# Moving a PSUM copy, one set of loads and the last stores in a Fourier-and-feed-forward kernel

## The chip, the cores and the metric

The kernel runs on one core of a Trainium2 chip. The metric is the device time of one execution in microseconds; several executions are taken and their median is compared. The profile is of one further execution.

## The reference

The input x has 8 batches of 3008 rows and 256 columns, in float32. Each batch gets a two-dimensional discrete Fourier transform, of which the real part is kept, and the result goes through a feed-forward layer with a hidden width of 2048 and the activation h cos(h):

```python
X = np.fft.fft(np.fft.fft(x, axis=1), axis=2).real
h = X.reshape(24064, 256) @ w_in        # 256 -> 2048
out = (h * np.cos(h)) @ w_out           # 2048 -> 256
```

## The kernel before, in words

The length 3008 is split into 47 x 64. For each batch a *transform* runs in two halves. The first half folds the rows of x (pairs of rows and pairs of columns are added and subtracted, so that cosines and sines need half the products), multiplies by a 47-point matrix (`first_half`, eight chunks c = 0 to 7 of the 64 residues) and writes the result to a buffer in DRAM (`store_z`). `load_z` reads it back in another order, and the second half (`second_half`, six groups g) multiplies by the 64-point matrix and gives a tile pq per group. The column transform is merged into the feed-forward weights (WC, WS), so pq goes straight into the feed-forward part.

The feed-forward part is a software pipeline of 384 steps t (8 batches, 6 groups, 8 slices fp of the hidden width, two blocks of 128 each). A step has seven matmuls of the second product into four PSUM accumulators M (`mm2`, L730), four of the first product into H (`mm1`, L640), and on the other engines: a seed of H from the norm row nb on ACT (`seed`, L610), a difference on DVE (`dve_h`, L656), rounding on ACT (`act_round`, L671), the fraction on DVE (`dve_frac`, L675), the sine on ACT (`act_sin`, L681), products on DVE (`dve_g`, L685) and three sums on DVE (`dve_s` with k = 0, 1, 2; L696 and L706). Each engine runs its instructions in the written order of the loop `for t in range(n + LAG + 1)` at the end of the kernel. Where a step is the last slice of its group, ACT copies the accumulators out (`take_m`), GpSimd adds them over the next four steps (`combine_m`, `add`), and seven and eight steps after that slice the two halves of the output tile are transposed on DVE and stored (`store_out`, L826 and L836).

The next batch's transform is laid between these steps. `transform(b)` enters its calls under the number of the step at whose end they run (`todo`), before whose sums they run (`between`), or beside which sum GpSimd starts (`aside`). For the second batch (b = 1) the loads of x (`load_later_x`, L178) stand at steps 2 to 5 for the first half of the columns p = 0 (tile xp0) and at 13 to 16 for p = 1. A call issues seven DMAs of up to seven rows; a fourth of a half has 28. Half of the calls read rows in ascending order, 8 KB at a stretch; the other half reads them in reversed order, 1 KB at a stretch. SP issues them, as it issues the edge rows xz (`load_ends`, L183), the norm row's way through DRAM (`second_half`, pq to nd, nd to nb, L495 and L496) and nearly all stores.

The first half for batches after the first is `first_half_later`. Chunks c = 0 and c = 4 begin with `middle_later`: eight or nine small matmuls (L341, L349) for column 128, the middle one, into columns 256 to 272 of the PSUM tile pz, and a copy of them on ACT into the tile mid (L352). Then come the wide products (L373 for c = 0, L385 for all) into columns 0 to 256 of pz and into a spare half of an accumulator, and ACT copies both and a few columns of mid into zs (L394 to L396). There are 7 such batches, so L352 runs 14 times.

The last step has its own ending. `combine_last` forms the last group's sums on DVE (L794 to L801), and `store_last` transposes them on PE (L811), copies them to ob (two buffers, in turn with those of `store_out`) and stores each half with four DMAs of 64 KB: six of the eight on SP, two on ACT (L818).

Of the kernel before, what the change touches and what calls it, by code (L numbers as in the profile page):

```python
# [30 lines left out]
LAG = 3  # L31
# [102 lines left out]
def kernel(  # L134
# [7 lines left out]
    nc = tc.nc  # L142
# [9 lines left out]
    x_r = x.rearrange("b (s2 s1) d -> b s2 s1 d", s1=64)  # L152
# [11 lines left out]
    def load_later_x(b, p, s, set_):  # L164
        i0 = 16 * set_ + 8 * p
        skip = 1 if s and i0 == 0 else 0
        cols = slice(64 - i0 - skip, 56 - i0, -1) if s else slice(i0, i0 + 8)
        to = xs[p].rearrange("r (s i d) -> r s i d", s=2, d=ND)[:, s, skip:8]
        for k in range(7):
            if s:  # L170
                r0, n = max(0, 40 - 7 * k), 5 if k == 6 else 7
                rows, p0 = slice(r0, r0 + n), 64 * set_ + _turned(46 - r0)
                part = slice(p0, p0 + n)
            else:
                n = 7 if k < 5 else 6
                rows, p0 = slice(k, N2, 7), 64 * set_ + 6 - k
                part = slice(p0, p0 + 7 * n - 6, 7)
            nc.sync.dma_start(out=to[part], in_=x_r[b, rows, cols])  # L178

    def load_ends(b):  # L180
        for set_ in range(2):
# [60 lines left out]
    mid = cpool.tile([128, NI], FP, tag="mid", name="mid")  # L242
# [92 lines left out]
    def middle_later(pz, p):  # L335
        pm = pz[64:128, 256:272]
        for set_ in range(2):
            i0 = 1 if set_ == p == 0 else 0
            for s in range(2):
                xm = xs[p].rearrange("r (s i d) -> r s i d", s=2, d=ND)[0:XL, s, i0:8, 128]  # L340
                nc.tensor.matmul(  # L341
                    pm[:, 8 * set_ + i0 : 8 * set_ + 8],
                    lhsT=weights(2 + set_, 0, XL),
                    rhs=xm,
                    start=s == 0,
                    stop=s == 1,
                )
        if p == 0:
            nc.tensor.matmul(  # L349
                pm[:, 0:1], lhsT=weights(4, 0, XL), rhs=xz[0:XL, 128:129], start=True, stop=True  # L350
            )
        nc.scalar.copy(  # L352
            out=mid[64:128].rearrange("y (h p i) -> y h p i", h=2, p=2)[:, :, p],
            in_=pm.rearrange("y (h i) -> y h i", h=2),
        )

    def clear_spare():
        nc.scalar.activation(
# [7 lines left out]
    def first_half_later(b, c):  # L366
        pz = psum("pz")
        spare = acc[live[0]][3][:, 256:512]
        if c % 4 == 0:
            middle_later(pz, c // 4)  # L370
        if c == 0:
            for e in range(2):
                nc.tensor.matmul(  # L373
                    pz[64 * e : 64 * e + 64, 0:128],
                    lhsT=weights(4 + e, 0, XL),
                    rhs=xfz[0:XL, 128 * e : 128 * e + 128],
                    start=True,
                    stop=True,
                )
        xf = xf1[c % 2]  # L380
        for e in range(2):
            for set_ in range(2):
                r0, r1 = 64 * set_, 64 * set_ + XT
                c0 = 128 if set_ == c == 0 else 0
                nc.tensor.matmul(  # L385
                    (spare if set_ else pz)[64 * e : 64 * e + 64, c0:256],
                    lhsT=weights(e, r0, r1),
                    rhs=xf[r0:r1, 256 * e + c0 : 256 * e + 256],
                    start=set_ == 0,
                    stop=True,  # L390
                    skip_group_check=set_ == 1,
                )
        zs = spool.tile([128, 512], FP, tag="zs", bufs=4, name="zs")
        nc.scalar.copy(out=zs[:, 256:512], in_=spare)  # L394
        nc.scalar.copy(out=zs[:, 0:256], in_=pz[:, 0:256])
        nc.scalar.copy(  # L396
            out=zs[64:128, 0:512:128].rearrange("y (h i) -> y h i", h=2),
            in_=mid[64:128].rearrange("y (h i) -> y h i", h=2)[:, :, 2 * c : 2 * c + 2],
        )
        zss[b, c] = zs  # L400
# [105 lines left out]
    todo = {}  # L506
# [3 lines left out]
    def transform(b):  # L510
        t0 = (b - 1) * NG * 8

        def at(o, *call):
            todo.setdefault(t0 + o, []).append(call)

        for p, o in enumerate((2, 13) if b == 1 else (-20, -9)):
            for k in range(4):
                at(o + k, load_later_x, b, p, k % 2, k // 2)
        at(4 if b == 1 else -16, load_ends, b)
        for c in range(NCH):  # L520
            o = 7 + 8 * (c // 2) + 2 * (c % 2)
            f = o + 2 + c % 2
            for e in range(2):
                aside.setdefault(t0 + o + e, []).append((fold_rows, b, c, e))
                between.setdefault(t0 + o + e + 1, []).append(
                    (fold_cols, xf1[c % 2], xs2[e], e)
                )
            at(f - 1, clear_spare)
            at(f, first_half, b, c)
            at(f + 1, store_z, b, c, 0)  # L530
            at(f + 1, store_z, b, c, 1)
        for e in range(2):
            between.setdefault(t0 + 7 + e, []).append((fold_cols, xfz, xz, e))
        at(38, load_z, b, 0)
        at(38, load_z, b, 1)
        for g, o in enumerate((42, 44, 46, 49, 52, 55)):
            at(o, second_half, b, g)
# [266 lines left out]
    def store_last(s, sg):  # L804
        cv = outs[s.b, s.grp].rearrange("p (m t) -> p m t", m=7)
        ob = spool.tile([128, 512], FP, tag="ob", bufs=2, name="ob")
        ov = ob.rearrange("t (h c j) -> t h j c", h=2, j=2)
        pos = [psum("po", "H").rearrange("t (z j c) -> t z j c", z=2, j=2)[:, 0] for _ in "ab"]
        for j in range(2):
            for h in range(2):  # L810
                nc.tensor.transpose(  # L811
                    pos[h][:, j], cv[:, 2 * sg + j, 128 * h : 128 * h + 128], ident
                )
        nc.scalar.copy(out=ov[:, 0], in_=pos[0])
        (nc.vector.tensor_copy if sg else nc.scalar.copy)(out=ov[:, 1], in_=pos[1])
        for t0, j, k, m in sorted(_runs(s.grp, sg)):
            h, r0 = divmod(32 * t0, 128)
            (nc.scalar if sg and h else nc.sync).dma_start(  # L818
                out=out_r[s.b, j, k : k + m, :],
                in_=ob[r0 : r0 + m, 256 * h : 256 * h + 256],  # L820
            )
# [78 lines left out]
    def step(t, last=None):  # L900
        s = steps[t] if 0 <= t < n else None
        return s if s is not None and (last is None or s.fp == 7) else None
# [10 lines left out]
    for t in range(n + LAG + 1):  # L913
        cur, prev, old, done = step(t), step(t - 1), step(t - 2), step(t - LAG)
        if cur:
            mm1(cur, 0)
            act_e(cur)
            if t == 0:
                spread_norm()
            if t in early:  # L920
                fold_weights(*early[t])
        if t - LAG - 1 == n - 1:
            combine_last(steps[n - 1])
            break
        if step(t - LAG - 1, True):
            take_m(step(t - LAG - 1), 1)
            combine_m(step(t - LAG - 1))
        if done:
            live[0] = (done.b, done.grp)
            mm2(done, 0)  # L930
        if old:
            dve_g(old, 0)
        if step(t + 1):
            seed(step(t + 1))
        if prev:
            dve_frac(prev, 0)
        if old:
            dve_g(old, 1)
        if prev:
            dve_frac(prev, 1)  # L940
            act_sin(prev)
        if old:
            dve_s(old, 0)
        for call in between.pop(t, ()):
            call[0](*call[1:])
        if done:
            dve_s(done, 2)
        ahead = dve_s(old, 1) if old else None
        if step(t - LAG, True):
            take_m(done, 0)  # L950
        if cur:
            mm1(cur, 1)
        if done:
            mm2(done, 1)
        if cur:
            dve_h(cur)
            act_round(cur, 0)
            act_round(cur, 1)
        for call in aside.pop(t, ()):
            beside(call[0](*call[1:]), ahead)  # L960
        if step(t - LAG - 4, True):
            store_out(step(t - LAG - 4), 0)
        if step(t - LAG - 5, True):
            store_out(step(t - LAG - 5), 1)
        for call in opening.pop(t, ()):
            call[0](*call[1:])
        for call in todo.pop(t, ()):
            call[0](*call[1:])
# [30 lines left out]
```

## Time and profile before

| what | value |
|---|---|
| median of 3 runs | 1966.43 us (1965.71 to 1967.67) |
| profiled execution | 1966.13 us, span 1964.4 us |
| granted TensorE clock, mean | 0.997 |
| PE, DVE, ACT, POOL busy | 1926.7, 1782.5, 1531.3, 379.6 us |
| matmuls of the second product, M (L730) | 7 per step, 384 steps |
| copies of the middle column (L352) | 14 x 0.17 us |
| loads of x by `load_later_x` (L178) | 392, on SP |

Times in the profile count from the start of the span. PE is the matmul unit, PEld its weight loads, DVE, ACT and POOL the vector, scalar and GpSimd engines; a q behind a name is the engine's queue, where DMAs are issued. A line of the timeline gives start, duration, engine, line of the kernel, operation and tiles; brackets hold the idle time just before and what ended it.

### The profile page before, as it was taken

How to read it: one execution, taken by the hardware profiler on the slowest of the kernel's cores; microseconds unless marked ns; L12 is line 12 of the kernel's file. 1: busy time of each engine (PE TensorE's matmuls, PEld its weight loads, DVE VectorE, ACT ScalarE, POOL GpSimd, SP SyncE). 2: the span in 40 equal slices, each digit the busy share in tenths (PEclk: the TensorE clock that was granted, in tenths of full speed). 3: DMA queues.
4: the chain of work that ended last, by engine and by line, in shares of the span. 5: the costliest groups of instructions: out<-in, count | busy, mean ns of one | idle time of the engine just before them, and what ended most of it. 6: DMA issues, size and time to landing. Idle time of an engine off the chain costs nothing.

```text
span 1964.4 us, 30495 instructions
## 1 busy us (share of the span) xinstructions
PE 1926.7 (98%) x9524; PEld 1690.4 (86%) x9524; DVE 1782.5 (91%) x3343; ACT 1531.3 (78%) x2881; POOL 379.6 (19%) x434
## 2 busy tenths in 40 slices
PE   7899999999999999999999999999999999999998
PEld 3788889888998889988898888988889888898887
DVE  4899998999899998999989999899999999999997
ACT  3687878877788788787877888778877888788775
POOL 2122202222022211222112221122211222111100
PEclk8999999999999999999999999999999999999999
DMA  6221130012200121101211122110231000110000
GB/s 198 95 57 37 49 91 25 19 38 68 64 23 22 41 75 52 25 24 46 80 39 26 26 52 76 33 31 22 54 84 29 24 23 24 53 29 10 12 22 22
DMA packets 159931, 89.31 MB, mean 45 GB/s; under 512 B 108298, under 2 KB 154114, under 8 KB 157302
## 3 DMA queue, kind: packets, MB, share of 16 engines
q1 hardware_dynamic: 158282, 86.27, 16.6%
q8 instruction: 76, 1.25, 0.3%
q10 hardware_dynamic: 1392, 1.05, 0.2%
q14 instruction: 85, 0.70, 0.1%
q0 software_dynamic: 96, 0.05, 0.0%
HBM read 50.04 MB, written 37.28 MB: 44 GB/s over the span
## 4 chain that ended last, share of the span: by engine, by line
PE 84%; DVE 7%; issue 3%; DMA 2%; ACT 2%; SPq 1%; DVEq 0%; ACTq 0%; POOL 0%; POOLq 0%
PE M L730 50%; PE H L640 30%; PE pb L473 2%; PE pz L385 2%; DVE r L685 1%; ACT r L671 1%; DVE S L696 1%; DVE h L656 1%; DMA xp<-in_x_dram 1%; DVE r L675 1%; DVE S L706 1%; DVE ob L826 1%; DMA zd<-zs 1%; DMA out_dram<-ob 1%; SPq L836 1%
## 5 line engine op out<-in xcount | busy, mean ns | idle before, releaser
L730 PE MATMUL M<-S,VX 128*128 128x256 f32 (+1 forms) x2304 | 612.3, 375 | 0.0
L730 PEld LDWEIGHTS M<-S,VX 128*128 128x128 f32 x2304 | 437.8, 190 | 49.9
L671 ACT ACTIVATE r<-H 128x512 f32<-128x512 f32 (+1 forms) x384 | 226.2, 589 | 264.8 <-DVE h L656 264.8
L681 ACT ACTIVATE r<-r 128x1024 f32<-128x1024 f32 (+1 forms) x384 | 394.8, 1028 | 21.6 <-DVE r L675 16.7
L640 PE MATMUL H<-pq,WC 128*128 128x256 f32 (+1 forms) x1536 | 394.6, 379 | 4.2 <-ACT H L610 4.2
L640 PE MATMUL H<-pq,WS 128*128 128x256 f32 (+1 forms) x1536 | 388.2, 375 | 0.6 <-ACT ew L651 0.5
L730 PE MATMUL M<-r,w 128*128 128x256 f32 (+1 forms) x1536 | 387.7, 375 | 0.0
L610 ACT ACTIVATE H<-nb,wn 128x256 f32<-128x256 f32 (+1 forms) x766 | 362.9, 474 | 18.4 <-DMA nb<-nd 4.5
L656 DVE TENSOR_TENSOR h<-ew,H 128x512 f32<-128x512 f32 (+1 forms) x384 | 258.7, 674 | 119.0 <-PE H L640 75.6
L640 PEld LDWEIGHTS H<-pq,WC 128*128 128x128 f32 x1536 | 283.3, 190 | 54.9 <-issue 11.1
L730 PEld LDWEIGHTS M<-r,w 128*128 128x128 f32 x1536 | 300.2, 196 | 27.4
L640 PEld LDWEIGHTS H<-pq,WS 128*128 128x128 f32 x1536 | 291.9, 190 | 36.6 <-ACT ew L651 1.8
L675 DVE SCALAR_TENSOR_TENSOR r<-r,H 128x512 f32<-128x512 f32 (+1 forms) x384 | 258.6, 673 | 28.0 <-ACT r L671 11.4
L651 ACT ACTIVATE ew<-H 128x512 f32<-128x512 f32 (+1 forms) x384 | 225.7, 588 | 56.4 <-PE H L640 47.3
L696 DVE TENSOR_TENSOR S<-r 128x512 f32<-128x512 f32 (+1 forms) x384 | 259.7, 676 | 0.1
L685 DVE SCALAR_TENSOR_TENSOR r<-H,r 128x512 f32<-128x512 f32 (+1 forms) x384 | 255.7, 666 | 4.4 <-ACT r L681 4.0
L782 POOL TENSOR_TENSOR cb<-cb,mr 128x256 f32<-128x256 f32 (+3 forms) x188 | 158.3, 852 | 519.5 <-DVE S L706 484.8
L675 DVE SCALAR_TENSOR_TENSOR r<-r,h 128x512 f32<-128x512 f32 (+1 forms) x384 | 258.3, 673 | 0.0
L685 DVE SCALAR_TENSOR_TENSOR r<-h,r 128x512 f32<-128x512 f32 (+1 forms) x384 | 258.0, 672 | 0.0
L671 ACT ACTIVATE r<-h 128x512 f32<-128x512 f32 (+1 forms) x384 | 236.0, 615 | 0.0
L300 POOL TENSOR_TENSOR xs<-xp 113x512 f32<-113x512 f32 x112 | 143.0, 1277 | 460.5 <-DVE S L706 403.7
L730 PE MATMUL M<-S,w 128*128 128x256 f32 (+1 forms) x768 | 225.8, 375 | 2.3 <-DVE S L706 2.3
(92 smaller groups left out, 1557.6 us busy)
## 6 DMA issues: line engine op xcount, KB each, us to landing
out_dram<-ob SPq DMA_DIRECT2D x728, 32.0 KB
xp<-in_x_dram SPq DMA_DIRECT2D x266, 56.0 KB
z<-zd SPq DMA_DIRECT2D x8, 1280.0 KB
zd<-zs SPq DMA_DIRECT2D x224, 40.0 KB
nb<-nd SPq DMA_DIRECT2D x40, 128.0 KB
zd<-zs SPq DMA_DIRECT2D x224, 8.0 KB
xp<-in_x_dram SPq DMA_DIRECT2D x56, 48.0 KB
xp<-in_x_dram SPq DMA_DIRECT2D x42, 49.0 KB
```

What stands on the lines that cost most here:

```text
L300: return nc.gpsimd.tensor_tensor(out=xs2[e][0:XL], in0=xv[:, 0], in1=xv[:, 1], op=ALU.subtract if e else ALU.add,)
L610: nc.scalar.activation(out=s.H[:, u * T : u * T + T], in_=s.nb[:, 0:T], func=AF.Copy, bias=0.25, scale=wn[:, f : f + 1],)
L640: nc.tensor.matmul(s.H[:, u * T : u * T + T], lhsT=W[:, 128 * f : 128 * f + 128], rhs=s.pq[:, e * T : e * T + T], start=False, stop=True, ...
L651: nc.scalar.mul(out=s.ew[:, 0 : 2 * s.T], in_=s.H[:, 0 : 2 * s.T], mul=2.0)
L656: nc.vector.tensor_tensor(out=s.h[:, 0 : 2 * T].rearrange("p (u t) -> p u t", u=2)[:, :, ::-1], in0=s.ew[:, 0 : 2 * T].rearrange("p (u t) ...
L671: nc.scalar.activation(out=r, in_=h, func=AF.Copy, bias=BIG, scale=1.0)
L675: nc.vector.scalar_tensor_tensor(out=r, in0=r, scalar=-BIG, in1=h, op0=ALU.add, op1=ALU.subtract)
L681: nc.scalar.activation(out=r, in_=r, func=AF.Sin, bias=0.0, scale=SIN_SCALE)
L685: nc.vector.scalar_tensor_tensor(out=r, in0=h, scalar=-0.25, in1=r, op0=ALU.add, op1=ALU.mult)
L696: return nc.vector.tensor_tensor(out=sv[:, 0:2], in0=gv[:, 2:3].to_broadcast([128, 2, T]), in1=gv[:, 0:4:3], op=ALU.subtract,)
L730: nc.tensor.matmul(acc[key][m // 2][:, 256 * (m % 2) : 256 * (m % 2) + T], lhsT=w, rhs=a, start=first, stop=s.fp == 7, skip_group_check=True,)
L782: return nc.gpsimd.tensor_tensor(out=o, in0=a, in1=b, op=ALU.subtract if less else ALU.add)
```

## The change

It has three parts.

1. The copy of the middle column into mid moves from the end of `middle_later` to behind the wide products of the same chunk.
2. For b = 1 and p = 0 the 28 DMAs of `load_later_x` are issued from GpSimd's queue in place of SP's, and at steps 0 to 3 in place of 2 to 5.
3. At the end of the kernel: the sum k = 2 of a step runs right behind its sum k = 1 from t = n on, not a step later; the second half of the group before the last (`store_out(..., 1)`, its transpose and its stores) moves from the end of step n - 1 to the end of step n + 1; and two of the stores of `store_last` for sg = 0 go from SP's queue to GpSimd's.

```diff
@@ load_later_x
-            nc.sync.dma_start(out=to[part], in_=x_r[b, rows, cols])
+            queue = nc.gpsimd if b == 1 and p == 0 else nc.sync
+            queue.dma_start(out=to[part], in_=x_r[b, rows, cols])
@@ middle_later
-        nc.scalar.copy(
-            out=mid[64:128].rearrange("y (h p i) -> y h p i", h=2, p=2)[:, :, p],
-            in_=pm.rearrange("y (h i) -> y h i", h=2),
-        )
@@ first_half_later, behind the wide products
+        if c % 4 == 0:
+            nc.scalar.copy(
+                out=mid[64:128].rearrange("y (h p i) -> y h p i", h=2, p=2)[:, :, c // 4],
+                in_=pz[64:128, 256:272].rearrange("y (h i) -> y h i", h=2),
+            )
@@ transform
-        for p, o in enumerate((2, 13) if b == 1 else (-20, -9)):
+        for p, o in enumerate((0, 13) if b == 1 else (-20, -9)):
@@ store_last
-            (nc.scalar if sg and h else nc.sync).dma_start(
+            queue = ((nc.scalar if sg else nc.gpsimd) if h else nc.sync)
+            queue.dma_start(
@@ the loop over t
-        if done:
+        if done and t <= n:
             dve_s(done, 2)
         ahead = dve_s(old, 1) if old else None
+        if old and t >= n:
+            dve_s(old, 2)
...
         if step(t - LAG - 5, True):
-            store_out(step(t - LAG - 5), 1)
+            if t == n - 1:
+                todo.setdefault(n + 1, []).append((store_out, step(t - LAG - 5), 1))
+            else:
+                store_out(step(t - LAG - 5), 1)
```

## The prediction

> **What bounds the kernel now.** The busy shares of the page come first: PE 1926.7 of 1964.4 us, so 37.7 us without a matmul in the whole span, and anything worth having must come out of those or out of the tail behind the last matmul. Second view: the waits between 130 and 1930 us, PE's own.
>
> ```profile
> PE pz L385 <- ACT mid L352: 6.3, 7, 1.0
> PE pz L373 <- ACT mid L352: 3.9, 6, 0.7
> ```
>
> These are the only waits of PE in 1800 us (columns: us in total, times, longest): all of them for the copy of the middle column (the first batch's c = 0 lies before 130 us). DVE in the same stretch waits 65.2 us for PE's H and 36.3 us for ACT's r, so DVE follows PE and has room. Third view, the timeline around one of these copies (start, duration, in brackets the idle time before and its releaser):
>
> ```profile
> 653.47 0.67 PE L341 MATMUL pz<-xp,V 113*64 113x8 f32 x8
> 654.14 0.62 ACT L671 ACTIVATE r<-h 128x512 f32<-128x512 f32 x1
> 654.79 0.17 ACT L352 COPY mid<-pz 64x16 f32<-64x16 f32 x1
> 655.01 0.43 PE L385 MATMUL pz<-xf,V 49*64 49x256 f32 x1 [0.87 <-ACT mid L352]
> 655.60 1.13 PE L640 MATMUL H<-pq,WC 128*128 128x256 f32 x4
> 655.74 0.37 ACT L394 COPY zs<-M 128x256 f32<-128x256 f32 x1 [0.78 <-PE M L385]
> ```
>
> PE has the small products ready at 654.14, ACT is still rounding (L671) until 654.76, copies, and only then PE writes other columns of the same PSUM tile. Then ACT in its turn waits 0.78 us for PE.
>
> Fourth view, the timeline of the first batch's start, where the slices of PE show the other hole:
>
> ```profile
> 69.81 3.60 SPq L178 DMA_DIRECT2D xp<-in_x_dram  x5
> 76.25 0.22 SPq L495 DMA_DIRECT2D nd<-pq  x1
> 77.77 2.40 SPq L178 DMA_DIRECT2D xp<-in_x_dram  x7
> 80.65 0.99 ACT L610 ACTIVATE H<-nb,wn 128x256 f32<-128x256 f32 x2 [4.50 <-DMA nb<-nd]
> 81.69 1.13 PE L640 MATMUL H<-pq,WC 128*128 128x256 f32 x4 [2.70 <-ACT H L610]
> 84.65 1.26 POOL L300 TENSOR_TENSOR xs<-xp 113x512 f32<-113x512 f32 x1 [56.83 <-DMA xp<-in_x_dram]
> 84.69 1.70 DVE L696 TENSOR_TENSOR S<-r 128x450 f32<-128x450 f32 x1
> 87.29 0.66 PE L730 MATMUL M<-S,w 128*128 128x225 f32 x2 [1.31 <-DVE S L706]
> ```
>
> SP issues 21 of the second batch's 28 loads (L178) and four edge loads from 56.9 to 76.2, and only then the two small transfers that carry the norm row nd to nb. pq was ready at 71.25 (L489: 70.66 + 0.59), so the row leaves 5.0 us late. The last seven loads land at about 84.6, and the fold that GpSimd starts late runs beside a DVE sum that takes 1.70 us here instead of its usual 0.62. PE loses 2.70 and 1.31 us.
>
> Fifth, the tail: the second transpose, PE's wait, and the queue that ends last.
>
> ```profile
> 1944.91 0.71 DVE L826 STREAM_TRANSPOSE ob<-cb 128x512 f32<-128x512 f32 x1
> 1948.99 0.71 PE L730 MATMUL M<-S,w 128*128 128x256 f32 x2 [1.01 <-DVE S L706]
> 1957.59 3.72 SPq L818 DMA_DIRECT2D out_dram<-ob  x6
> 1958.86 1.44 ACTq L818 DMA_DIRECT2D out_dram<-ob  x2
> ```
>
> The chain of waits runs through DVE from 1939.4 to 1948.9, both transposes in it; then 28 matmuls without a gap; then the last sums. SP's six stores end at 1961.31, SP waits 1.5 us for them, and 1.6 us of closing follow.
>
> **The change, part by part.** The profiled execution took 1966.13 us round its span of 1964.4; the median of three is 1966.43, 0.30 more. A measurement of this kernel can tell about 0.2% (3.9 us) from no change.
>
> *Middle column.* Removed: all 14 waits, 4.7 us at L373 (7) and 6.3 us at L385 (7): 11.0 us. The copy stays on ACT, in the same place of ACT's order, 14 x 0.17 us, and now waits for the wide products. That wait is not new: ACT already waits 13.5 us (14 times) for L385 before the next copy, L394. In the example PE would go on at 654.14, be through the wide products at 654.73 (655.60 less 0.87), and ACT, free at 654.76, copies mid at once and starts L394 near 654.93. Against PE's next matmuls ACT is then about 0.2 us later than now. The cover is ACT's slack: L651 ends at 657.37 where PE needs it at 658.29, 0.9 us of room. Were it gone, the price is 14 x 0.17 = 2.4 us. Ends: 8.6 to 12.2 us (the weight loads' waits, 5.3 + 6.9). Taken: -11.0.
>
> *Loads from GpSimd.* The 28 loads leave SP (median issue 0.67 us there) and go to GpSimd, two steps earlier. GpSimd's order has nothing else between its last fold copy (26.76 + 0.71) and the memsets that clear xz, so they can start near 27.5. SP then reaches nd as soon as pq is ready, 71.3; with the 4.4 us that the pair took from 76.25 to 80.65, nb is there at 75.7. ACT would seed at 76.15, behind L651: no wait, 2.70 us gained. The fold needs xp0 at about 78.5, where DVE's sum of that step ends; then it no longer stands beside L696, and the 1.31 us go too. Sum -4.0, if the loads land by 78.5.
>
> Do they? The only GpSimd DMAs of the trace:
>
> ```profile
> 3.31 1.68 POOL L195 DMA_DIRECT2D xp<-in_x_dram  x3 [0.76 <-DVE xp L245]
> xp<-in_x_dram POOLq DMA_DIRECT2D x1, 15.0 KB, 5.9
> ```
>
> 0.56 us each for 16 runs of 1 KB, landing at most 5.9 us after issue. Half of the 28 read whole 8 KB rows (7 runs): 0.56 us as lower bound. The others read single reversed rows, up to 56 runs: 0.56 if a DMA costs the same whatever it holds, 1.96 if it goes by runs. Total 15.7 to 35 us, so the last lands between 49 and 69. Even by bytes (56 KB against 16) all 28 would take 55 us and land by 88. I take by runs, the dearer, as their shapes are not those of the row; it still arrives in time. The memset of xz now stands behind 14 of these loads, and SP's edge loads wait for it: done by about 46, where SP comes there at 56.8.
>
> What it costs: 1.5 MB move earlier, from 27.5 on, while the first batch's path is itself made of DMAs.
>
> ```profile
> 30.00:32.00 2.00, 2.00 (x6) 0.95 (x5) 0.00 (x0) 0.78 (x2) 0.00 (x0) 1.00 1.06 368
> 36.62 1.16 PE L473 MATMUL pb<-BJ,z 128*128 128x128 f32 x8 [2.13 <-DMA z<-zd]
> ```
>
> The last columns of the first line are the DMA share (full) and 368 GB/s. PE waits for z until 36.62 behind this. GpSimd can add between 9.1/1.96 = 5 loads (0.26 MB) and 9.1/0.56 = 16 loads (0.90 MB) before that: 0.7 to 2.4 us at 368 GB/s if every byte is in the way, 0 if none is. Part of the stretch is not full (0.25 from 32 to 34), so I take +1.2, ends 0 and 2.4. The Trainium skill ("DMA: Bandwidth & Descriptors", section "Issuing engines are not separate DMA queues") says that all queues run on the same 16 DMA engines and another issuer saves only issue time. By that rule the gain here could be SP's issue time alone and the moved bytes are paid in full; the sum would be that of rival two. The full share agrees with the shared engines.
>
> *Tail.* One transpose (0.71) moves off t = n-1 to behind the last sums, and PE's wait of 1.01 shrinks by it: -0.7. In its new place it ends near 1952.3 by DVE's order (five ops and three sums from 1947.2), before DVE's next work at 1953.6: hidden behind PE's matmuls. The sum k = 2 taken one step earlier only swaps places on DVE (0.34 us, PE needs it 3 us later). But the transpose's eight stores come with it: 8 x 0.60 on SP, 1952.3 to 1957.1, so SP is free when the first last-store is ready (1957.59 less 0.7). The last tile shares its buffer with them (two in rotation): its copy waits for them to land, 1957.1 + 1.5 = 1958.6, 1 us later than it could. SP's last two stores then end near 1960.2 and land near 1961.7, against 1962.8. The two on GpSimd, ready at 1957.1, issue in 1.1 (as above) to 4 us and land 4.7 to 5.9 us after issue: 1961.9 to 1964. Taken -0.5; ends -1.1 and +1.3.
>
> Sum: -11.0 - 4.0 + 1.2 - 0.5 = -14.3: 1951.8 for the profiled execution, 1952.1 beside the median.
>
> **The rivals.**
>
> *Two: the start gives nothing.* The early loads delay z by the full 2.4, and PE idles long enough at 34.5 to 36.6 that the low granted clock (0.50 in the windows 40 to 46) lasts longer; another 1.6 us eats the 4.0. For: the full DMA share. Against: the large weight loads already hold it, and GpSimd issues slowly. 1966.43 - 11.0 - 0.5 = 1954.9.
>
> *Three: the middle's gain doesn't come.* PE stands at the next point where ACT is behind (the change then doesn't do what it says). Against: ACT's 13.5 us of waiting in the same place. 1966.43 - 3.3 = 1963.1.
>
> *Four, slower: GpSimd can't issue while DVE works.* Then its loads use DVE's idle time: 15.3 us between 28 and 54 (26 less the busy 10.7 of the windows), nothing from 54 to 78 where DVE is 98% busy. If reversed loads also cost 1.96, 20 us of issuing are left when DVE stands still for the fold at about 79; the last lands near 79 + 20 + 5.9 = 105, and PE waits for the fold (1.27) and DVE's sums (1.1) from 83.3 (87.29 less the 1.31 and 2.70 it now waits) to 107.4: 24 us. Sum: -11.0 - 4.0 + 24 + 1.2 - 0.5 = +9.7: 1976.1. It turns against the change once the last load lands behind 95, 2.2 us for each load. The trace's three GpSimd DMAs met an idle DVE for most of their time, so it neither shows nor excludes this. The Trainium skill ("SBUF — State Buffer", section "Who interferes with whom") has DVE lock GpSimd out of writing descriptors only in copies, casts and tensor-scalar forms; by it this kernel's sums would not starve the loads. No run here shows it.
>
> **How the numbers follow.** Forecast 0.64, rival two 0.20, three 0.07, four 0.09. The forecast with its bounds reaches from 1966.43 - 12.2 - 4.0 - 1.1 = 1949.1 to 1966.43 - 8.6 - 4.0 + 2.4 + 1.3 = 1957.5; that takes in rival two and leaves three and four out, 0.16. The lower end needs every bound at once, so I set 1949.6. Faster by over 0.2% are the first two, and three's upper half is at the edge: 0.85; same 0.06; slower 0.09.
>
> **What would show it.** Right: no wait of PE for L352 or for any ACT copy at L373 and L385; the 28 loads on GpSimd's queue between 27 and 63; nd at 71 and no idle time before L610 of step 8; L300 first at 78 to 80; PE's z wait at 36.6 later by 1 us; one transpose behind the last sums, PE's wait before the tail's L730 near 0.3. Wrong: loads of over 2 us on GpSimd, POOL L300 waiting for xp beyond 80, a new wait of PE on M or H behind the wide products, or GpSimd's two stores landing last.

## The result, and the profile after

The changed kernel takes 1953.05 us (median of 6 runs, 1951.37 to 1953.86) against 1967.18 us for the kernel before (6 runs, 1965.71 to 1969.24): a ratio of 0.9926, 95% interval 0.9913 to 0.9939. That is 14.1 us less. The profiled execution took 1953.48 us round a span of 1951.7, where before it was 1966.13 round 1964.4, so the two traces that are compared here differ by 12.7 us. Lines behind an insertion have new numbers: L178 is now L179, L300 L301, L341 L342, L385 L382, L352 L391, L473 L475, L495 L497, L610 L612, L640 L642, L730 L732, L818 L821, L826 L829. The 28 loads that the change moves are four calls of seven.

Four places that both traces have, in us from the start of the span, show where the time went.

| place | before | after | after less before |
|---|---|---|---|
| first product with z (pb) | 36.62 | 40.31 | +3.7 |
| the same for the second group | 69.57 | 74.88 | +5.3 |
| first small products of the middle column, c = 0 | 92.44 | 93.03 | +0.6 |
| last wide product | 1663.8 | 1651.7 | -12.1 |
| end of the span | 1964.4 | 1951.7 | -12.7 |

Between these two traces the start loses 0.6 us where the forecast had it win 2.8, the middle gains 12.7 where it had 11.0, and the tail 0.6. By them, that the total came out near the forecast is partly luck: two errors have opposite signs. The start's 0.6 holds for these two executions only: c = 0 stands at 93.58 in one kernel below that has its loads as in before (e1) and at 88.92 in another (e4), by the clock.

**The middle.** PE's waits between 120 and 1945 us (columns: us in total, times, longest). There is no copy of ACT among them, and nothing has taken its place; both lines belong to the tail.

```profile
PE po L813 <- DVE cb L799: 0.9, 1, 0.9
PE M L732 <- DVE S L708: 0.6, 1, 0.6
```

The timeline round the same c = 4 as in the prediction:

```profile
649.55 0.63 PE L342 MATMUL pz<-xp,V 113*64 113x8 f32 x8
650.11 0.43 PE L382 MATMUL pz<-xf,V 49*64 49x256 f32 x1
650.23 0.62 ACT L673 ACTIVATE r<-h 128x512 f32<-128x512 f32 x1
650.70 1.13 PE L642 MATMUL H<-pq,WC 128*128 128x256 f32 x4
650.87 0.17 ACT L391 COPY mid<-pz 64x16 f32<-64x16 f32 x1
651.14 0.37 ACT L396 COPY zs<-M 128x256 f32<-128x256 f32 x1
```

The wide products (L382) now follow the small ones while ACT still rounds, the copy to mid runs beside PE's next work, and zs is copied right behind. From the small products to the next H product it takes 1.15 us, against 2.13 before: 0.98 less, where PE's row of before had a wait of 0.87 in its brackets. All of it lies between the first small product and the first wide one, which are 0.56 us apart now (649.55, 650.11) and were 1.54 apart (653.47, 655.01). The bracket counts from the end of the small products, and without the wait the first wide product starts a little before that end. Over the 13 places behind 140 us the gain is 11.65 us, 0.90 each.

**The start.** PE's waits in the first 120 us, and the timeline of the rows that the prediction followed:

```profile
PE pb L475 <- DMA z<-zd: 6.1, 1, 6.1
PE H L642 <- ACT H L612: 1.9, 3, 0.8
```
```profile
26.74 4.14 POOL L179 DMA_DIRECT2D xp<-in_x_dram  x8
32.70 3.53 POOL L179 DMA_DIRECT2D xp<-in_x_dram  x6 [1.82 <-DMA xp<-in_x_dram]
36.58 5.33 POOL L179 DMA_DIRECT2D xp<-in_x_dram  x10
40.31 2.08 PE L475 MATMUL pb<-BJ,z 128*128 128x128 f32 x8 [6.14 <-DMA z<-zd]
76.59 0.23 SPq L497 DMA_DIRECT2D nd<-pq  x1
81.37 0.98 ACT L612 ACTIVATE H<-nb,wn 128x256 f32<-128x256 f32 x2
83.46 1.27 POOL L301 TENSOR_TENSOR xs<-xp 113x512 f32<-113x512 f32 x1 [35.70 <-DVE S L708]
84.15 1.02 PE L642 MATMUL H<-pq,WC 128*128 128x256 f32 x4
```

Read it from below. The H product of step 8 (L642) and the seed (L612) have no idle time in brackets, where before PE stood 2.70 us and ACT 4.50 there; the fold (L301) waits for DVE's sum and no longer for its data. These are the two waits that the loads were to remove. But z arrives late: PE stands 6.14 us for it, not 2.13, and GpSimd has issued 14 loads by 36.3, before SP issues the last of z's DMAs (36.95). And the first products with z take 2.08 us, not 1.16, and the granted clock is low behind that gap. The windows of after show it (stretch, busy us and counts of PE, PEld, DVE, ACT and POOL, granted clock, DMA share, GB/s). They also show that the DMA engines are less than half busy while z is on its way, 0.44 from 32 to 36 (a mean of the 16; single engines can't be seen in it):

```profile
32.00:36.00 4.00, 2.17 (x6) 0.62 (x4) 1.55 (x4) 1.75 (x3) 3.26 (x6) 1.00 0.44 136
36.00:40.00 4.00, 0.00 (x0) 0.00 (x0) 2.57 (x7) 0.00 (x0) 4.00 (x12) 0.65 0.56 142
40.00:44.00 4.00, 2.87 (x10) 2.53 (x11) 0.00 (x0) 0.70 (x2) 2.08 (x5) 0.50 1.09 311
44.00:48.00 4.00, 4.00 (x10) 2.23 (x9) 1.03 (x3) 0.60 (x2) 2.10 (x4) 0.50 1.11 163
```

**The tail.** PE's wait is down from 1.01 to 0.57 us, the transpose lies behind the last sums beside PE's matmuls, and the queues end at 1948.7 (SP) and 1948.98 (ACT).

```profile
1936.40 0.71 PE L732 MATMUL M<-S,w 128*128 128x256 f32 x2 [0.57 <-DVE S L708]
1940.03 0.71 DVE L829 STREAM_TRANSPOSE ob<-cb 128x512 f32<-128x512 f32 x1
1945.54 3.16 SPq L821 DMA_DIRECT2D out_dram<-ob  x4
1945.56 1.14 POOL L821 DMA_DIRECT2D out_dram<-ob  x2 [17.00 <-ACT ob L817]
1947.18 0.39 ACT L816 COPY ob<-po 128x256 f32<-128x256 f32 x1 [1.91 <-DMA out_dram<-ob]
1947.70 1.28 ACTq L821 DMA_DIRECT2D out_dram<-ob  x2
```

### The profile page after: what moved, and what is told of

Same layout as the page of the kernel before. It is cut to its first block, busy times and chain, and to the rows that moved or that the text cites. A ratio compares the mean times of both kernels' runs of the same rounds, so it can differ in the third digit from the quotient of the medians.

```text
span 1951.7 us, 30532 instructions
## 1 busy us (share of the span) xinstructions
PE 1924.2 (99%) x9524; PEld 1691.9 (87%) x9524; DVE 1781.7 (91%) x3343; ACT 1530.5 (78%) x2881; POOL 396.0 (20%) x464
## 4 chain that ended last, share of the span: by engine, by line
PE 96%; DMA 1%; DVE 1%; issue 0%; ACT 0%; SPq 0%; ACTq 0%; POOL 0%; DVEq 0%; POOLq 0%
PE M L732 58%; PE H L642 34%; PE pb L475 2%; PE pz L382 2%; DMA zd<-zs 1%; DMA xp<-in_x_dram 1%; PE pz L342 0%; PE pw L545 0%; PE pz L425 0%; SPq L839 0%; PE M L382 0%; DVE r L687 0%; DMA z<-zd 0%; PE pz L370 0%; DVE S L698 0%
## 5 line engine op out<-in xcount | busy, mean ns | idle before, releaser
L732 PE MATMUL M<-S,VX 128*128 128x256 f32 (+1 forms) x2304 | 612.4, 375 | 0.0
L732 PEld LDWEIGHTS M<-S,VX 128*128 128x128 f32 x2304 | 437.8, 190 | 49.8
L642 PE MATMUL H<-pq,WC 128*128 128x256 f32 (+1 forms) x1536 | 394.7, 379 | 1.9 <-ACT H L612 1.9
L642 PE MATMUL H<-pq,WS 128*128 128x256 f32 (+1 forms) x1536 | 387.8, 375 | 0.6 <-ACT ew L653 0.5
L732 PE MATMUL M<-r,w 128*128 128x256 f32 (+1 forms) x1536 | 387.7, 375 | 0.0
L612 ACT ACTIVATE H<-nb,wn 128x256 f32<-128x256 f32 (+1 forms) x766 | 363.0, 474 | 13.9
L642 PEld LDWEIGHTS H<-pq,WC 128*128 128x128 f32 x1536 | 283.6, 190 | 52.5 <-ACT r L673 15.8
L732 PEld LDWEIGHTS M<-r,w 128*128 128x128 f32 x1536 | 300.3, 196 | 27.2
L642 PEld LDWEIGHTS H<-pq,WS 128*128 128x128 f32 x1536 | 291.7, 190 | 36.0 <-ACT ew L653 1.8
L301 POOL TENSOR_TENSOR xs<-xp 113x512 f32<-113x512 f32 x112 | 143.1, 1278 | 440.9 <-DVE S L708 440.9
L732 PE MATMUL M<-S,w 128*128 128x256 f32 (+1 forms) x768 | 225.6, 375 | 0.6 <-DVE S L708 0.6
```

The costliest lines, as they stand in the source:

```text
L301: return nc.gpsimd.tensor_tensor(out=xs2[e][0:XL], in0=xv[:, 0], in1=xv[:, 1], op=ALU.subtract if e else ALU.add,)
L612: nc.scalar.activation(out=s.H[:, u * T : u * T + T], in_=s.nb[:, 0:T], func=AF.Copy, bias=0.25, scale=wn[:, f : f + 1],)
L642: nc.tensor.matmul(s.H[:, u * T : u * T + T], lhsT=W[:, 128 * f : 128 * f + 128], rhs=s.pq[:, e * T : e * T + T], start=False, stop=True, ...
L732: nc.tensor.matmul(acc[key][m // 2][:, 256 * (m % 2) : 256 * (m % 2) + T], lhsT=w, rhs=a, start=first, stop=s.fp == 7, skip_group_check=True,)
```

## The experiments

The theory after the two traces: the middle gives all of the gain, the loads win at two waits what was forecast but lose it again because they start before z's way through DRAM is done, and the tail is too small to see. The rivals: part of the gain belongs to the loads or the tail, or the z delay has another cause.

**One part at a time.** Four kernels from before: the first has only the copy moved, the second only the loads, the third only the tail, the fourth the first and the third.

```diff
@@ e1_mid, from before: this alone
@@ middle_later
-        nc.scalar.copy(
...
@@ first_half_later, behind the wide products
+        if c % 4 == 0:
+            nc.scalar.copy(
...
@@ e2_loads, from before: this alone
+            queue = nc.gpsimd if b == 1 and p == 0 else nc.sync
-        for p, o in enumerate((2, 13) if b == 1 else (-20, -9)):
+        for p, o in enumerate((0, 13) if b == 1 else (-20, -9)):
@@ e3_tail, from before: this alone, with the store_out of step n - 1 at n + 1
+            queue = ((nc.scalar if sg else nc.gpsimd) if h else nc.sync)
-        if done:
+        if done and t <= n:
+        if old and t >= n:
+            dve_s(old, 2)
@@ e4_mid_tail, from after: the loads taken back
-            queue = nc.gpsimd if b == 1 and p == 0 else nc.sync
-        for p, o in enumerate((0, 13) if b == 1 else (-20, -9)):
+        for p, o in enumerate((2, 13) if b == 1 else (-20, -9)):
```

> Only the copy of the middle column moves. By the ledger read from the two traces (the stretch with these chunks is 12.5 us shorter, more than the 11.0 us of PE's idle time) this alone is worth 12 to 12.7 us, ratio near 0.9937. By the sum on record it is worth 11.0 us, ratio 0.9944. If part of the gain needed the other edits, it is under 10 us.

> Only the 28 loads move to GpSimd's queue. By the ledger the start as a whole is no faster, between 1 us slower and 1 us faster: PE's wait for z grows from 2.1 to about 6 us, and the waits of 2.7 and 1.3 us further on go. By the sum on record it is 2.8 us faster, with z's wait near 3.3 us.

> Only the last sums, the last transpose and the last stores are reordered. Both the ledger and the sum on record say 0.5 us faster, under what a time can tell; the profile should show PE's wait for the last sums fall from 1.0 to 0.6 us and the last tile's copy wait some 1.9 us for the stores of the buffer before.

> The change without its loads. By the ledger 12.5 to 13.3 us faster than before, so as fast as the whole change or up to 0.6 us faster than it. By the sum on record 11.5 us faster, 2.8 us slower than the whole change.

| kernel | median us | ratio to before, 95% |
|---|---|---|
| e1_mid | 1953.77 | 0.9923 (0.9910 to 0.9935) |
| e2_loads | 1965.12 | 0.9986 (0.9977 to 0.9995) |
| e3_tail | 1967.21 | 0.9992 (0.9983 to 1.0001) |
| e4_mid_tail | 1953.68 | 0.9918 (0.9906 to 0.9931) |

Before ran at 1968.92 us beside them. The copy alone brings a gain as large as the whole change's. The stretch from the product with z near 140 us to the last wide product is 1522.9 us in before, e2 and e3, and 1511.2 in after, e1 and e4, with no difference above 0.1: the middle's gain depends on nothing else. PE's waits of e1 in the first 1950 us show that the two waits of the start stay when the loads stay on SP, with z in time:

```profile
PE H L641 <- ACT H L611: 4.4, 4, 2.9
PE pb L474 <- DMA z<-zd: 2.2, 1, 2.2
PE M L731 <- DVE S L707: 2.3, 2, 1.3
```

In e2 both are gone and the first z product moves to 41.12 us. Over the four kernels without the early loads it stands at 36.62, 36.45, 35.47 and 35.52, over after, e2 and e5 with them at 40.31, 41.12 and 39.81: 4.4 us later in the mean. The tail alone can't be told from nothing by its time; from the last wide product to the end its trace has 299.9 us, before 300.6.

The times of the single parts don't add up neatly. By their ratios e1 is 15.1 us faster (12.8 to 17.7), e2 2.8 (1.0 to 4.5) and e3 1.6, 19.5 in all, and the whole change 14.6 by its ratio. Within their intervals they can add up, but e1's time gives more than the 12.7 us that its trace accounts for between c = 0 and the last wide product. e2 is the clearest case: its 11 executions are faster than before's 21, and by the same 2.8 us that the prediction's sum has for the loads, while its trace has the product near 140 us 1.5 us later than before. That trace is one of e2's slower executions (1967.04, median 1965.12), before's trace a fast one of before (1966.13, median here 1968.92). Beside the other two parts the loads bring nothing that the times show: the whole change has a ratio of 0.9926, e4, which lacks them, 0.9918. So whether the loads, issued this early, win or lose as a whole is not settled. One execution of a kernel differs from the next by the clock (below), and how much of the rest that is stays open.

**The loads held back.** e5_all is the whole change once more. e6_gate_pq and e7_gate_ew1 add one copy of a single element to GpSimd's order ahead of the loads; the element belongs to the first pq (e6: z has then arrived) or to a tile of the second feed-forward step (e7: the loads then stand at steps 2 to 5, where DVE is busy). In e8_eighth the loads start as early as in after and are as many, but each brings one column of rows out of eight; seven eighths of the second batch's first half are left out.

```diff
@@ e6_gate_pq, e7_gate_ew1, from after
+    held = cpool.tile([1, 1], FP, tag="held", name="held")
+    def hold(k):
+        src = ready[0, 0][0] if k == 0 else steps[k].ew
+        nc.gpsimd.tensor_copy(out=held, in_=src[0:1, 0:1])
@@ e6_gate_pq: at(0, hold, 0) ahead of the loads; e7_gate_ew1: at(1, hold, 1), loads from step 2
@@ e8_eighth, from after
+            if b == 1 and p == 0:
+                few = slice(cols.start, cols.start + cols.step if cols.step else cols.start + 1, cols.step)
+                queue.dma_start(out=to[part][:, 0:1], in_=x_r[b, rows, few])
+                continue
```

> The whole change once more, beside the three that follow. All theories: ratio to before 0.991 to 0.994, PE's wait for z near 6 us in the profile.

> The whole change, but GpSimd first copies one element of the first pq, so that its 28 loads start near 39 us, when z has been read, and not at 27. If the loads' traffic is what holds z back, PE's wait for z falls from 6 to 2 to 3 us and the time by 2 to 4 us against the whole change; the waits for nb and for the fold stay away (loads landed by 66, needed near 78). If z's wait has another cause (the order of the issues, chance of the launch), it stays near 6 us and the time the same.

> As the gate on pq, but held until ACT's copy of H in step 1 (near 49 us), and the calls at steps 2 to 5 again. GpSimd then issues while DVE is 85 to 98% busy: if DVE kept GpSimd from issuing, a load would take over 1 us instead of 0.55, and the fold would wait for xp beyond 80 us. If not, 0.55 us each, landing by 72 to 78, and the time is that of the gate on pq or up to 1.5 us less, as the weight loads and the norm row's way are free of this traffic too.

> The whole change, but each of the 28 loads brings one of its eight columns of rows only (7/8 of the second batch's first half is left out): as many GpSimd DMAs, an eighth of the bytes. If bytes in the way hold z back, PE's wait for z is 2 to 3 us. If the number of DMAs or GpSimd's issuing does, it stays near 6 us. By the issue cost by runs the reversed loads would go from 2.0 to 0.3 us; by a fixed cost all stay at 0.55.

| kernel | median us | ratio to before, 95% |
|---|---|---|
| e5_all | 1953.14 | 0.9923 (0.9909 to 0.9936) |
| e6_gate_pq | 1945.68 | 0.9886 (0.9871 to 0.9900) |
| e7_gate_ew1 | 1948.90 | 0.9903 (0.9889 to 0.9916) |
| e8_eighth | 1951.40 (one run) | |

Holding the loads until z is there takes 7.5 us off the changed kernel (the intervals of e5 and e6 lie apart), where 2 to 4 were expected. Between the traces of e5 and e6 it is 9.1 us: 4.3 until the first product with z, and 4.8 more until that of the second group (34.79 us further on in e5, 30.03 in e6), where e5 has the low clock and e6 hasn't. The other executions of e6 are not all so: half of them are 3.2 to 4.2 us slower (below). The timeline of e6 shows the order that results: z, the held copy, the loads, and the fold, which has its data and stands nine microseconds earlier than in after.

```profile
35.52 1.16 PE L477 MATMUL pb<-BJ,z 128*128 128x128 f32 x8 [1.78 <-DMA z<-zd]
37.26 0.18 POOL L516 COPY held<-pq 1x1 f32<-1x1 f32 x1 [10.53 <-ACT pq L488]
37.49 4.13 POOL L179 DMA_DIRECT2D xp<-in_x_dram  x8
74.13 1.27 POOL L303 TENSOR_TENSOR xs<-xp 113x512 f32<-113x512 f32 x1 [19.87 <-DVE S L716]
```

The chain of waits says what was late. First e5, then e6 (start, us, transfer):

```profile
25.56 6.66 DMA zd<-zs
32.30 4.23 DMA zd<-zs
36.58 3.19 DMA z<-zd
```
```profile
25.93 5.16 DMA zd<-zs
31.16 1.45 DMA zd<-zs
32.67 2.81 DMA z<-zd
```

All three transfers of z's way are slower beside the loads, by 1.5, 2.8 and 0.4 us. e8 was to tell bytes (a wait of 2 to 3 us) from the number of DMAs (near 6), and its one run gives neither: with an eighth of the bytes PE still waits 4.95 us for z. By that wait 1.2 of the 4.3 us between e5 and e6 go with the bytes. By the start at 37.62 it is 2.2, but e8's first half also ended 1.0 us earlier than e5's. So a quarter to a half of the delay goes with the bytes. The rest is not the time of bytes in the way: in e8 the last store to zd lands only at 34.39, though the DMA share is 0.04 to 0.09 in each microsecond from 32 to 35, and little moves in the whole window:

```profile
32.00:36.00 4.00, 0.68 (x2) 0.00 (x0) 2.99 (x9) 0.69 (x1) 3.88 (x12) 1.00 0.21 20
```

Whether the rest hangs on the number of DMAs or on their small pieces was not told apart. The Trainium skill ("DMA: Bandwidth & Descriptors", section "Issuing engines are not separate DMA queues") says that another issuer brings no new DMA engines. By that rule the early loads must be paid for in z's way; a delay of 4.4 us agrees, though its size doesn't follow from the bytes. It also says that only issue time is saved. That time is not small here: with z at 35.52 in both, e6 reaches the first small products of c = 0 at 83.69 and e4 at 88.92, 5.2 us apart, because the norm row and the fold no longer stand behind the loads in SP's order.

e7 settles rival four for this kernel's work on DVE. Its timeline issues 15 loads in a row, the later of them where DVE is nearly full in the windows:

```profile
50.45 8.15 POOL L179 DMA_DIRECT2D xp<-in_x_dram  x15
```
```profile
54.00:58.00 4.00, 3.18 (x13) 1.93 (x12) 3.70 (x8) 3.73 (x8) 4.00 (x7) 1.00 0.64 151
58.00:62.00 4.00, 3.96 (x20) 3.37 (x20) 3.92 (x9) 3.20 (x6) 3.59 (x8) 1.00 0.91 280
```

0.54 us a load on average, and seven in the 4 us in which DVE is 92% busy, is about the price beside a DVE that is mostly idle (8 in 4.14 us above, DVE 28% busy): sums, differences, fractions and products on DVE don't keep GpSimd from issuing. The Trainium skill ("SBUF — State Buffer", section "Who interferes with whom") names only other forms of DVE's work as doing so, and e7 agrees. By its time e7 missed: it was to be as fast as e6 or up to 1.5 us faster, and its median lies 3.2 above (the two intervals overlap). In its trace z comes as early (35.94), but the second group's product stands 34.1 us behind it, with a clock of 0.50 between 40 and 48, against 30.0 in e6.

**The clock and the last buffer.** Within one kernel the time goes with the mean granted clock: e6 ran at 1943.6 and 1944.1 us with 0.998, at 1947.3 and 1947.8 with 0.995. The question was whether the stretch at 0.50 behind the z wait is worth a filler. e9_all_busy puts six dummy matmuls without use into that gap of the changed kernel, e10_gate_busy two into e6's; e11_gate_ob3 gives e6's output tile a third buffer, and e12_gate_busy_ob3 has both.

```diff
@@ e9_all_busy from after (6), e10_gate_busy and e12_gate_busy_ob3 from e6 (2), before second_half(0, 0)
+    pd = psum("pd", "M")
+    for i in range(6):
+        nc.tensor.matmul(pd, lhsT=LCS[:, 0:128], rhs=LCS[:, 0:512], start=i == 0, stop=i == 5)
@@ e11_gate_ob3, e12_gate_busy_ob3 from e6, in store_last and store_out
-        ob = spool.tile([128, 512], FP, tag="ob", bufs=2, name="ob")
+        ob = spool.tile([128, 512], FP, tag="ob", bufs=3, name="ob")
```

> The whole change, with six matmuls of 128x512 without use in the gap in which PE waits for z (about 5.2 of its 6 us). They separate the two parts of the start's loss: z is as late as before, but PE isn't idle. If the low granted clock behind the gap (0.50 from 38 to 50 us) is a consequence of the gap, it goes, and the time falls by 3 to 5 us to about 1949. If the clock falls for another reason, the time stays or grows by up to 1 us.

> The gate on pq with two such matmuls (1.7 us) in the gap of 1.8 us. The runs of the gate alone fell into two groups, 1943.6 to 1944.1 and 1947.3 to 1947.8. If the low clock behind the gap, which comes in some executions only, makes the second group, all runs now lie near 1943.5 to 1944.5. If the groups have another cause, both are still there.

> The gate on pq with three output buffers in place of two, so that the last tile's copy need not wait for the eight stores moved in front of it (1.9 us on ACT and DVE). The last stores on ACT's queue go out 1.5 to 1.9 us earlier; if they end the kernel it is 0.8 to 1.5 us faster. SP's own queue is busy until about 1.2 us later, so if SP ends it, 0 to 0.6 us.

> Gate, filled gap and three output buffers together: by the sums 1942.5 to 1944, the fastest of all; if the filled gap or the buffers bring nothing, as the gate alone, near 1945.7.

| kernel | median us | ratio to before, 95% |
|---|---|---|
| e9_all_busy | 1949.63 | 0.9913 (0.9897 to 0.9928) |
| e10_gate_busy | 1945.95 | 0.9888 (0.9874 to 0.9901) |
| e11_gate_ob3 | 1947.81 | 0.9900 (0.9885 to 0.9915) |
| e12_gate_busy_ob3 | 1945.33 | 0.9886 (0.9872 to 0.9899) |

In e9 the clock stays at 1.00, as one line of its timeline and one of its windows show:

```profile
38.64 1.05 PE L475 MATMUL pb<-BJ,z 128*128 128x128 f32 x8
```
```profile
40.00:44.00 4.00, 3.49 (x13) 2.16 (x14) 1.45 (x4) 1.32 (x4) 1.34 (x3) 1.00 1.11 213
```

The first product with z comes 1.2 us earlier than in e5 (38.64 against 39.81; SP issues z's last DMA at 34.36, not at 36.58, and PE then is still at the filler), the product near 140 us 4.7 us earlier (135.41 against 140.13); so the low clock behind the gap costs about 3.5 us of its own, and the median of e9 lies 3.5 us below e5's, though the two intervals overlap. The Trainium skill ("TensorE: Matmul & The Clock Gate", section "Part 1: The HAM clock gate (the 'warmup' mystery)") has the clock halved after an idle window of some 3.4 us, which may fall differently in each run; the 6.1 us gap of after and its filling in e9 agree. It doesn't cover all: before has 0.50 behind a wait of 2.13, e4 and e6 1.00 behind 1.64 and 1.78, e7 0.50 behind 1.54, e10 0.79 where the wait was only 0.21, and e12 0.52 where PE did not wait for z at all. First e10, then e12:

```profile
37.23 1.16 PE L477 MATMUL pb<-BJ,z 128*128 128x128 f32 x8 [0.21 <-DMA z<-zd]
40.00:44.00 4.00, 4.00 (x12) 2.02 (x11) 1.52 (x4) 0.89 (x2) 3.89 (x8) 0.79 0.86 271
```
```profile
36.04 1.16 PE L477 MATMUL pb<-BJ,z 128*128 128x128 f32 x8
40.00:44.00 4.00, 4.00 (x6) 1.76 (x7) 1.32 (x4) 0.90 (x2) 2.82 (x6) 0.52 0.71 206
```

By the clock records of the traces, which have only 1.0 and 0.5, the low stretch behind z lasts 13.7 us in all four kernels with early loads and no filler (after, e2, e5, e8), 10.2 in e1, e3 and e7, 6.8 in before and e12, 3.4 in e10 and e11, and nothing in e4, e6 and e9, always a whole multiple of 3.41. So the long wait always brought the longest stretch; among the others it came out differently, though before, e1, e3 and e4 have the same instructions up to there.

Two dummies bring nothing beside e6 (e10, e12). They were to unite e6's two groups of times, but e10's executions still lie at 1944.1, 1945.0, 1946.9 and 1947.0, and its trace still has a low stretch. What sets the clock at that point is not settled. The third buffer does in the trace what it should: the copy that waited 1.91 us for the landing of the stores now waits 0.45 for PE, and the end comes 299.3 us after the last wide product, not 300.1. The time doesn't show these 0.8 us: e11's median lies above e6's, and the intervals of the two overlap.

```profile
1938.45 0.38 ACT L824 COPY ob<-po 128x256 f32<-128x256 f32 x1 [0.45 <-PE po L821]
```

## Why the prediction was right, and where it was not

**Middle, forecast -11.0, measured -11.65 for 13 places and -12.7 with all that lies between c = 0 and the last wide product.** The mechanism was right: no wait took the place of the old one, ACT's slack was enough, and rival three is out (e1). The mis-sized term is the price of one wait. The prediction took PE's matmul rows (4.7 + 6.3) and kept the weight loads' rows (5.3 + 6.9 = 12.2) as the far end. A place gave 0.90 us, 14 of them 12.5, so the far end was the better reading.

**Loads, the two waits: forecast -4.0, measured -4.7.** From the second group's product with z to the H product the time fell from 12.12 to 9.27, from there to the small products of c = 0 from 10.75 to 8.88. Right in place, and 0.7 us more in size.

**Loads, the delay of z: forecast +1.2 with ends 0 and 2.4, measured +4.4, outside its ends.** This is the step that failed. The bound divided the bytes of 5 to 16 loads by 368 GB/s. 14 loads were issued by then, so the count was inside the bounds; but from 32 to 36 us, where z is held up, the DMA engines of after are 0.44 busy and move 136 GB/s, and e8 leaves half of the delay or more with an eighth of the bytes. So the delay is not the time that the bytes take at full rate; what the rest of it is stays open. All three transfers of z's way were stretched, the way to DRAM most (e5 against e6), where the bound had looked at the last one's wait alone.

**Loads, the price of one: 0.56 to 1.96, taken 1.96; measured 0.50 to 0.67 us, median 0.56, over all 28, of 7 runs and of up to 56.** "By runs" was wrong, and so the last load was issued at 47.8 us and not near 63. At 1.96 only 5 loads would have stood before z, and 14 did.

**What the sum didn't have: the clock.** The low granted clock stood in rival two, not in the forecast. Rival two came half true: in the traces the delay and the clock took back what the loads won, and the time is nevertheless near the forecast's, since the middle gave 1.5 to 1.7 us more. That the total came so near to the forecast's 14.3 us is partly luck.

**Tail, forecast -0.5, measured -0.6 in the trace** (from 300.61 to 300.05 us behind the last wide product). PE's wait shrank to 0.57, not 0.3, and the buffer cost 1.91 us, not 1; both small, and the two stores on GpSimd took 1.14 us for issue, the lower of the two bounds.

**Rival four** is refuted by e7: the loads go out at about the same price beside a busy DVE.

## What to carry to other kernels

Put the small read of an accumulator behind the last writes to the same accumulator, when the engine that reads it is busy with something else: it cost 0.9 us each time here, and the price is read from the weight loads' waits rather than the matmuls'. Moving loads to an idle queue also lets them start as soon as their buffer is free; look for a transfer on the critical path in the stretch where they will now run, and hold them behind it with a dependency, which here was worth 7.5 us of 1953, part of it by the clock. Check each part of a change alone, since a total that fits the forecast can hide a gain and a loss.

## What was not expected of the hardware

Issuing one load from GpSimd's queue took 0.50 to 0.67 us in after, with 7 runs of 8 KB as with up to 56 runs of 1 KB, and 0.49 to 0.53 with an eighth of the data (e8). After eight of them GpSimd stood 1.82 us in after until one had landed; in e7 it issued 15 without such a stop. z's way through DRAM came 4.4 us later beside these loads, though the DMA engines were only 0.44 busy in the mean from 32 to 36 (after). One wait of PE of some microseconds near the start can be followed by a granted clock of 0.50 for up to 13.7 us (before from 39.8 to 46.6, after from 37.2 to 50.8), which cost 3.5 us in e5 against e9. The same kernel is 3 to 9 us slower in executions where its mean clock is 0.992 to 0.995 and not 0.998 (before: 1962.69 with 0.998, 1969.6 to 1971.5 with 0.992). What decides between the two where the wait is below 2.2 us was not found.
